# The opening of a Fourier filter with a layer pair behind it: filter read directly, first unit with plain products, weight conversion moved

## The chip, the core and the metric

The kernel runs on one core of a Trainium2 chip. The metric is the time of one execution on the device in microseconds; three runs of the kernel before gave 2558.02, 2558.45 and 2562.6, median 2558.45. The profile is of one further execution. Its engines are TensorE (PE, with PEld for its weight loads), VectorE (DVE), ScalarE (ACT), GpSimd (POOL) and SyncE (SP); SP and POOL issue nearly all transfers.

## The reference

Eight sequences of 3008 tokens with 256 channels are filtered in the frequency domain, and every token then goes through two layers with an ELU between them:

```python
X = np.fft.rfft(x, axis=1)                       # x: (8, 3008, 256)
F = (filt_r + 1j * filt_i)[None, :, :]           # 1505 frequencies x 256
y = np.fft.irfft(X * F, n=x.shape[1], axis=1).astype(np.float32)
x = y.reshape(8 * 3008, 256)
h = x @ w_in                                     # 256 -> 2048
g = np.where(h > 0.0, h, np.exp(np.minimum(h, 0.0)) - 1.0)
return (g @ w_out).astype(np.float32)            # 2048 -> 256
```

The two weight matrices arrive as 64-bit floats, the rest as 32-bit floats.

## The kernel before, in words

**The transform.** 3008 = 47 x 64. A sequence is read as 47 rows of 64 tokens, and row n1 is paired with row 47 - n1, which makes 24 pairs (`H`), in six tiles of four pairs. The first step (`a_first` for batch 0, `a_unit` after that) is a transform of length 64 in a tile, by products with a table. The second is the transform of length 47 across the rows (`b_first`, `b_unit`); it gives the frequencies in groups. In each group DVE multiplies by the filter (`products`, four steps of 128 x 512). Then come the way back (`bi_first`, `bi_unit`), a trip through DRAM (`y_write`, `y_read`; the scratch tensor is `yd`), and a last product with a table (`n_unit`, tile `psn`), after which the rows lie transposed for the layers.

**The layers.** Work is cut into units: a batch has six (m = 0 to 5), each of four row blocks of at most 256 tokens, and a unit runs in four quarters q, each with 512 of the 2048 hidden features. One quarter of one unit is one step of the big loop, here called a quarter; there are 8 x 6 x 4 = 192. A quarter's two products are done as 2 x 2 block products by a scheme with seven products in place of eight (Strassen's, in Winograd's form): `up_steps` gives seven steps of PE for the first layer, `down_steps` seven for the second, and the second runs one quarter behind. Sums of input blocks (`n_sums`), of weight blocks (`w_sums`, four DVE additions a pair of weight tiles) and of ELU outputs go with it. The ELU of a block is two ACT steps (Relu, Exp) and one DVE step. First-layer results lie in four PSUM banks that are handed out and given back in the order of the program (`bank`, `banks`).

**The weights.** 16 tiles of 128 x 512 (k = 4q + j; j = 0, 1 of the first layer, 2, 3 of the second) are fetched as pairs of 32-bit words (`w_fetch`, 512 KB each) and converted by hand: `w_split` (two DVE steps cut mantissa and exponent out of the upper word), `w_float` (four ACT steps: low word, mantissa, two for the exponent), `w_join` (DVE: sign, sum, product into the weight tile).

**The opening, batch 0.** In the order of the program: POOL fetches weight tiles 1 to 3 and then sorts the filter, DRAM to DRAM, into `fd` with 28 transfers (`f_arrange`), later reads it into the tile `ff` with 16 (`f_read_first`, one pair for each of eight groups). SP fetches tile 0, the six x tiles and their tables, further weight tiles in between. PE does `a_first` for each x tile as it comes; its results go to the tiles `zt`. `t_first` transposes them for a group (32 transposes ahead of the loop, 8 behind each of the first four groups). The filter loop runs over g = 0 to 9: `b_first(g)`, products, `bi_first(g - 2)`, `y_write_first(g - 2)`. Tiles 0 to 6 are converted ahead of the loop, 7 to 10 in it, 8 to 13 partly and wholly behind it, 12 to 15 to their end during the first unit. Tiles of x, of `zq`, `rq` and of the result buffers serve as room for weights in between.

**The order behind it** is written out by hand: `plan` names, for each quarter and each of four places in it, what is put there (place 2 and 3 inside the first half, 0 in the middle, 1 behind the quarter's end); `opens` names quarters that begin with a second-layer step. Every engine runs its instructions strictly in this order. `f_pairs` builds, in four pieces during quarters 1 to 4, a second DRAM copy of the filter (`fp`) for batches 1 to 7. The first step of batch 1 (`x_unit`, `a_unit`, `z_write`) stands in quarters 2 to 4, its second (`b_unit`, which needs `z_read`) at the end of quarter 6.

[...]

Of the kernel before, what the change touches and what calls it, by code (L numbers as in the profile page):

```python
# [26 lines left out]
P = 128  # L27
# [14 lines left out]
def _make_tables():  # L42
# [78 lines left out]
    tw = np.ascontiguousarray(tn[:, 0:8].reshape(4, K2, 8, 2, 2, 32).transpose(1, 0, 2, 4, 3, 5)).reshape(P, 8, P)  # L121
# [12 lines left out]
def kernel(  # L134
# [49 lines left out]
    fd = fdp.tile([NG, 2, 48, 2, 2, D], FP32, name="fd")  # L184
# [105 lines left out]
    def t_first(g):  # L290

        t = t2s[0, g] = t4p.tile([P, 4, D], FP32, tag="t4", name="tf") if g % 4 > 1 else t2[:, g % 4]
        for j in range(2):
            i = j + 2 * (g % 2 if g < 4 else 0)
            ps = psO.tile([P, 2, 256], FP32, tag="po%d" % i, name="po%d" % i)
            for u in range(2):
                k = 4 * g + 2 * j + u
                for dh in range(2):
                    nc.tensor.transpose(ps[0:ROWS, u, ts(dh, P)], zt[k // 16][dh][:, ts(k % 16, ROWS)], eye)  # L299
            nc.scalar.activation(out=t[0:ROWS, 2 * j:2 * j + 2, :], in_=ps[0:ROWS], func=AXT.Copy)  # L300
# [19 lines left out]
    def f_read_first(g, t):  # L320
        for a, r in enumerate((LO, HI)):
            nc.gpsimd.dma_start(t[r].rearrange("p c u d -> p (c u d)"), fd[g, a].rearrange("q c u d -> q (c u d)"))
# [12 lines left out]
    def products(re, im, f, sr, si, p, q):  # L335

        nc.vector.tensor_tensor(out=sr, in0=re, in1=f[:, 0], op=ALU.mult)
        nc.vector.tensor_tensor(out=si, in0=re, in1=f[:, 1], op=ALU.mult)
        nc.vector.scalar_tensor_tensor(out=p, in0=im, scalar=-1.0, in1=f[:, 1], op0=ALU.mult, op1=ALU.mult)
        nc.vector.tensor_tensor(out=q, in0=im, in1=f[:, 0], op=ALU.mult)  # L340
# [144 lines left out]
    def y_read(b, m, *parts):  # L485
        t = t4s[b, m] = t4p.tile([P, 4, D], FP32, tag="t4", name="t4")
        for k in parts or (slice(0, K2),):
            if whole(b, m):
                r = slice(4 * k.start, 4 * k.stop)
                nc.sync.dma_start(t[r], yds[b].rearrange("k (p i) d -> (k p) i d", p=4)[r, 4 * m:4 * m + 4, :])  # L490
                continue
            for r in range(2):
                o = 64 * r
                nc.sync.dma_start(t[o + 2 * k.start:o + 2 * k.stop].rearrange("q i d -> q (i d)"),
                                  yds[b][k.start + r:k.stop:2].rearrange("k (p i) d -> k p (i d)", p=4)
                                  [:, :, 4 * m * D:4 * m * D + 4 * D])
# [9 lines left out]
    def n_whole(b, m):  # L506
# [10 lines left out]
        b11, b12, b21, b22 = rows  # L517
        t = yp.tile([P, 2, 256], FP32, tag="yb", name="yb")[:, :, 0:h]
# [42 lines left out]

    COMBO = {1: 0, 2: 2, 3: 6, 4: 3, 5: 4, 6: 5, 7: 1}
# [5 lines left out]
    def up_steps(b, m, q):  # L568

        h = half(m)  # L570
# [82 lines left out]
    def down_steps(b, m, q):  # L653
        h = half(m)
# [82 lines left out]
    def w_fetch(k, queue=nc.gpsimd):  # L737
        q, j = divmod(k, 4)

        if k in (3, 4, 14, 15):  # L740
            wd = t2[:, k % 11 - 3].rearrange("p u d -> p (u d)")
        elif k == 10:
            wd = t1p.tile([P, XC, D], FP32, tag="t1", name="wd").rearrange("p u d -> p (u d)")
        elif k in (6, 7, 8, 9):
            wd = xp.tile([P, 2, 2, D], FP32, tag="xc", name="wd").rearrange("p k u d -> p (k u d)")
        else:
            wd = fbufs[{5: 0, 11: 0, 12: 1, 13: 2}.get(k, k)].rearrange("p c u d -> p (c u d)")
# [14 lines left out]
    def w_split(k):  # L762
        m, e, f, l = wts[k] = wtmp[{9: 2, 10: 1, 11: 0, 12: 3, 13: 4, 15: 5}.get(k, k % 2)]
# [4 lines left out]
    def w_float(k, *parts):  # L768
        m, e, f, l = wts[k]
        ef = e.bitcast(FP32)  # L770
        steps = ((l, wds[k][:, :, 0], AXT.Identity, 2.0 ** -52, 0.0), (f, m, AXT.Identity, 2.0 ** -20, 1.0),
                 (ef, e, AXT.Relu, -8.0, edges[:, 0:1]), (e, ef, AXT.Relu, -1.0, edges[:, 1:2]))
        for i in parts or range(4):
            o, x, func, scale, bias = steps[i]
            nc.scalar.activation(out=o, in_=x, func=func, scale=scale, bias=bias)

    def w_join(k, parts=(0, 1)):
        q, j = divmod(k, 4)
        m, e, f, l = wts[k]
        if 0 in parts:  # L780
            nc.vector.scalar_tensor_tensor(out=e, in0=wds.pop(k)[:, :, 1], scalar=0x80000000, in1=e,
# [320 lines left out]
```

## Time and profile before

| | |
|---|---|
| median of three runs | 2558.45 us |
| profiled execution, its own time / span | 2560.57 / 2558.6 us |
| PE, DVE, ACT busy | 99%, 81%, 60% |
| last rows of x landed | 39.63 us |
| filter loop's first product (psr) | 48.43 us |
| first unit's first product (psn) | 85.68 us |
| end of the second batch's psa behind quarter 3 | 137.37 us |

The span is cut into stages by landmarks in the timeline of PE: the first step's products have the tile `psa`, the transposes and the way back `po`, the second step `psr` and `psi`, the last table product `psn`, the layers' first products `phs`, `pha`, `phd`. L numbers are lines of the kernel before. In the table of stretches the columns are: the stretch and its length, then busy time and count for PE, PEld, DVE, ACT and POOL, then the granted clock, the share of the DMA engines and GB/s. In a timeline, square brackets hold idle time ahead of the row and what ended it.

### The profile page before, as it was taken

The page shows a single profiled execution, that of the slowest core. Times are in us where ns is not written, and L with a number is a line of the kernel's source. Part 1 is how long each engine was busy: PE and PEld are TensorE (multiplying, and loading weights), DVE is VectorE, ACT ScalarE, POOL GpSimd, SP SyncE. Part 2 cuts the span into 40 slices and gives each one's busy share as a digit, 9 for nine tenths or more (in the row PEclk, how much of TensorE's full clock was granted, in tenths as well). Part 3 has the DMA queues.
Part 4 walks back from the last instruction along what each step waited for, and adds up shares of the span by engine and source line. Part 5 has one row for each costly group of instructions (what it writes and reads, how often), then busy time and mean ns, then how long its engine had stood idle before and what let it go on. Part 6 is the DMA issues. An engine that isn't in the chain of part 4 may idle for free.

```text
span 2558.6 us, 43997 instructions
## 1 busy us (share of the span) xinstructions
PE 2522.3 (99%) x16690; PEld 2164.8 (85%) x16690; DVE 2066.1 (81%) x3577; ACT 1544.9 (60%) x2716; POOL 160.2 (6%) x315
## 2 busy tenths in 40 slices
PE   6999999999999999999999999999999999999999
PEld 4788889888898888988889888888888888898888
DVE  6978887788878888788887888778897788876766
ACT  7765556655566565665566656565656655555555
POOL 5001000010000000000000000000100011000000
PEclk9999999999999999999999999999999999999999
DMA  9672213522133231433215231343213322110010
GB/s 281 178 189 65 62 39 81 130 67 69 44 102 100 67 69 40 121 82 72 57 44 150 64 80 36 77 122 81 60 41 85 84 63 69 36 46 18 19 28 17
DMA packets 228295, 200.62 MB, mean 78 GB/s; under 512 B 127174, under 2 KB 200406, under 8 KB 228084
## 3 DMA queue, kind: packets, MB, share of 16 engines
q1 hardware_dynamic: 213588, 166.93, 26.6%
q0 software_dynamic: 14000, 30.44, 4.3%
q8 instruction: 131, 2.15, 0.4%
q14 instruction: 80, 0.66, 0.1%
q10 hardware_dynamic: 496, 0.46, 0.1%
HBM read 125.86 MB, written 78.12 MB: 80 GB/s over the span
## 4 chain that ended last, share of the span: by engine, by line
PE 96%; DMA 2%; DVE 1%; ACT 0%; issue 0%; SPq 0%; DVEq 0%; ACTq 0%
PE po L665 45%; PE phs L583 25%; PE phd L583 13%; PE pha L583 6%; PE psn L535 2%; PE psa L237 2%; PE pf L388 1%; PE pv L460 1%; DMA xc<-in_x_dram 1%; DMA x<-in_x_dram 0%; PE po L333 0%; PE po L299 0%; DMA yd<-t 0%; PE psr L333 0%; DMA t<-yd 0%
## 5 line engine op out<-in xcount | busy, mean ns | idle before, releaser
L665 PE MATMUL po<-g,wo 128*128 128x256 f32 (+1 forms) x5376 | 1317.6, 377 | 0.0
L665 PEld LDWEIGHTS po<-g,wo 128*128 128x128 f32 x5376 | 1010.7, 190 | 165.8 <-issue 49.6
L594 ACT ACTIVATE g<-phs 128x512 f32<-128x512 f32 (+1 forms) x576 | 338.8, 588 | 737.1 <-PE phs L583 735.7
L601 ACT ACTIVATE e<-e 128x512 f32<-128x512 f32 (+1 forms) x768 | 477.2, 621 | 24.4
L605 DVE SCALAR_TENSOR_TENSOR g<-e,g 128x512 f32<-128x512 f32 (+1 forms) x576 | 387.3, 672 | 13.8 <-ACT e L601 13.4
L591 DVE TENSOR_TENSOR g<-phd,g 128x512 f32<-128x512 f32 (+1 forms) x384 | 258.7, 674 | 165.1 <-ACT e L601 107.7
L583 PE MATMUL phs<-y,wi 128*128 128x256 f32 (+1 forms) x1536 | 388.4, 375 | 0.0
L583 PE MATMUL phd<-y,wi 128*128 128x256 f32 (+1 forms) x1504 | 380.3, 375 | 0.0
L600 ACT ACTIVATE e<-g 128x512 f32<-128x512 f32 (+1 forms) x576 | 354.4, 615 | 34.1 <-DVE g L591 26.7
L583 PEld LDWEIGHTS phs<-y,wi 128*128 128x128 f32 x1536 | 291.9, 190 | 33.4 <-ACT g L594 0.2
L583 PEld LDWEIGHTS phd<-y,wi 128*128 128x128 f32 x1504 | 284.8, 190 | 35.1 <-DVE g L591 2.6
L605 DVE SCALAR_TENSOR_TENSOR g<-e,phs 128x512 f32<-128x512 f32 (+1 forms) x192 | 129.9, 677 | 115.5 <-ACT e L601 115.5
L583 PE MATMUL phs<-yt,wi 128*128 128x256 f32 (+1 forms) x768 | 193.8, 375 | 0.9 <-ACT g L594 0.9
L583 PE MATMUL phs<-yb,wi 128*128 128x256 f32 (+1 forms) x768 | 193.8, 375 | 0.6 <-ACT g L594 0.6
L583 PE MATMUL pha<-yb,wi 128*128 128x256 f32 (+1 forms) x736 | 185.9, 375 | 0.0
L600 ACT ACTIVATE e<-phs 128x512 f32<-128x512 f32 (+1 forms) x192 | 112.3, 585 | 111.9 <-PE phs L583 111.8
L591 DVE TENSOR_TENSOR g<-pha,g 128x512 f32<-128x512 f32 (+1 forms) x192 | 129.3, 673 | 45.5 <-PE pha L583 45.5
L583 PEld LDWEIGHTS phs<-yt,wi 128*128 128x128 f32 x768 | 145.7, 190 | 17.8 <-ACT g L594 1.2
L583 PEld LDWEIGHTS phs<-yb,wi 128*128 128x128 f32 x768 | 143.9, 190 | 19.3 <-ACT g L594 1.0
L327 POOL DMA_DIRECT2D fall<-fp x224 | 110.5, 501 | 721.9 <-DVE r L433 696.7
L583 PEld LDWEIGHTS pha<-yb,wi 128*128 128x128 f32 x736 | 139.8, 190 | 16.1
L642 DVE TENSOR_TENSOR g<-g,g 128x512 f32<-128x512 f32 (+1 forms) x192 | 130.7, 681 | 6.7
(170 smaller groups left out, 2066.3 us busy)
## 6 DMA issues: line engine op xcount, KB each, us to landing
yd<-t SPq DMA_DIRECT2D x127, 192.0 KB
t<-yd SPq DMA_DIRECT2D x92, 256.0 KB
z<-t SPq DMA_DIRECT2D x84, 256.0 KB
fall<-fp POOLq DMA_DIRECT2D x224, 96.0 KB, 3.0
t<-z SPq DMA_DIRECT2D x224, 96.0 KB
out_dram<-o SPq DMA_DIRECT2D x624, 32.0 KB
xc<-in_x_dram SPq DMA_DIRECT2D x84, 128.0 KB
xc<-in_x_dram SPq DMA_DIRECT2D x161, 64.0 KB
```

Source lines behind the costliest of these rows:

```text
L237: nc.tensor.matmul(p[o:o + 64, u, :], w[r, u, o:o + 64], src[r, u, :], start=True, stop=True)
L327: nc.gpsimd.dma_start(t[32 * a:32 * a + 24].rearrange("p c u d -> p (c u d)"), fp[g, a].rearrange("q c u d -> q (c u d)"))
L388: nc.tensor.matmul(pf[p][1][32 * a:32 * a + 32, js, :], fb[r, v, :], t2[r, js, a, :], start=True, stop=True, tile_position=(32 * p, 32 * a))
L535: nc.tensor.matmul(o, t[r, i - 4 * m, ds(dh * P + 64 * c, 64)], w[r, i - 4 * m, :], start=True, stop=True)
L583: nc.tensor.matmul(ps[:, a, 0:h], w_in[q][:, COMBO[n], a, :], y[n], start=start and a == 0, stop=True, skip_group_check=True)
L591: nc.vector.tensor_tensor(out=g[o], in0=i0, in1=i1, op=ALU.add)
L594: nc.scalar.activation(out=g[o], in_=i0, func=AXT.Copy)
L600: nc.scalar.activation(out=e, in_=src, func=AXT.Relu, scale=-1.0)
L601: nc.scalar.activation(out=e, in_=e, func=AXT.Exp, scale=-1.0)
L605: nc.vector.scalar_tensor_tensor(out=g[n], in0=es[n], scalar=1.0, in1=src, op0=ALU.subtract, op1=ALU.max)
L642: nc.vector.tensor_tensor(out=b12, in0=b22, in1=b12, op=ALU.subtract)
L665: nc.tensor.matmul(po[i][:, u, 0:h], w_out[q][:, COMBO[n], a, :], g[n][:, a, :], start=q == 0 and a == 0 and n in (1, 3, 6, 4), stop=True, ...
```

## The change

Four things are changed together.

1. The filter no longer goes through `fd`. `f_read_first(k, n)` reads frequencies k to k + n - 1 of each half straight from the inputs into `ff`, for (0, 4), (4, 4) and (8, 8): 26 transfers on SP, behind x and the two tables, and 12 of seven rows on POOL. A group now holds frequencies 2g, 2g + 1 and 16 + 2g, 16 + 2g + 1; transposes, the table `tw` and `y_read` of batch 0 follow that order (four transfers in place of two for m = 2 to 5). `f_pairs` reads the inputs too.
2. Weights: tiles 0 to 2 come on POOL first of all, tile 3 on SP behind x tile 3, tiles 4 to 8 behind the filter, 9 during the loop, 10 to 15 behind the read of yd. The conversion has one ACT step less (`w_join` does the mantissa's scaling). Ahead of the loop tiles 0 to 3 are converted, none in it; tile 4 begins before the last eviction, 4 to 7 and half of 8 are behind the loop, the rest are in quarters 0 to 2.
3. The first unit (b = 0, m = 0) is done with eight plain block products per layer and quarter in two sets of steps (`plain_ups`, `plain_downs`). It needs no sums. The weights' sums go to quarters 2 to 7, all on DVE; one set was on POOL before.
4. The first step of batch 1 moves to quarters 3 to 5.

```diff
-    def f_read_first(g, t):
-        for a, r in enumerate((LO, HI)):
-            nc.gpsimd.dma_start(t[r].rearrange("p c u d -> p (c u d)"), fd[g, a].rearrange("q c u d -> q (c u d)"))
+    def f_read_first(k, n):
+        for c, src in enumerate((filt_r, filt_i)):
+            for a in range(2):
+                o, row, e = 64 * a, 16 * a + k, 1 if k == a == 0 else 0
+                nc.sync.dma_start(ff[o:o + 48:2, c, k:k + n].rearrange("q k d -> q (k d)"),
+                                  raw(src, row, [[64 * D, 24], [1, n * D]]))
+                for j, m, queue in ((0, 16, nc.sync), (16, 7, nc.gpsimd)):
+                    queue.dma_start(ff[o + 2 * j + 1:o + 2 * (j + m):2, c, k + e:k + n],
+                                    raw(src, 64 * (j + 1) - row - e, [[64 * D, m], [-D, n - e], [1, D]]))
...
+    def plain_ups(b, m, q):
...
+        def step(i, j, k):
+            if k == 0:
+                held[i, j] = bank("php")
+            n, ps = held[i, j]
+            for a in range(2):
+                nc.tensor.matmul(ps[:, a, 0:h], w_in[q][:, 2 * k + i, a, :], rows[k][j],
+                                 start=k == a == 0, stop=True, skip_group_check=True)
+            if k == 1:
+                src = ps[:, :, 0:h]
+                e = ep.tile([P, 2, 256], FP32, tag="e", name="e")[:, :, 0:h]
+                nc.scalar.activation(out=e, in_=src, func=AXT.Relu, scale=-1.0)
+                nc.scalar.activation(out=e, in_=e, func=AXT.Exp, scale=-1.0)
+                nc.vector.scalar_tensor_tensor(out=g[i, j], in0=e, scalar=1.0, in1=src, op0=ALU.subtract, op1=ALU.max)
+                banks.append(held.pop((i, j))[0])
...
+    def plain_downs(b, m, q):
...
+        def step(i, j, e):
+            for a in range(2):
+                nc.tensor.matmul(po[e][:, j, 0:h], w_out[q][:, 2 * i + e, a, :], g[i, j][:, a, :],
+                                 start=q == i == j == a == 0, stop=True, skip_group_check=True)
...
-        steps = ((l, wds[k][:, :, 0], AXT.Identity, 2.0 ** -52, 0.0), (f, m, AXT.Identity, 2.0 ** -20, 1.0),
-                 (ef, e, AXT.Relu, -8.0, edges[:, 0:1]), (e, ef, AXT.Relu, -1.0, edges[:, 1:2]))
+        steps = [(l.bitcast(FP32), l, AXT.Identity, 2.0 ** -52, 1.0),
+                 (ef, e, AXT.Relu, -8.0, edges[:, 0:1]), (e, ef, AXT.Relu, -1.0, edges[:, 1:2])]
...
-            nc.vector.tensor_tensor(out=f, in0=f, in1=l, op=ALU.add)
+        nc.vector.scalar_tensor_tensor(out=f, in0=m, scalar=2.0 ** -20, in1=l, op0=ALU.mult, op1=ALU.add)
...
-            f_arrange()
-            w_fetch(0, nc.sync)
...
+            for k, n in ((0, 4), (4, 4), (8, 8)):
+                f_read_first(k, n)
...
-                if g == 1:
-                    w_split(9)
-                if g == 2:
-                    w_join(7)
-                    w_sums(7, nc.gpsimd)
-                if g == 5:
-                    w_split(10)
-                if 3 <= g < 6:
-                    w_fetch(g + 8, nc.sync)
+                if g == 3:
+                    w_fetch(9)
+                for k in {NG: (4,), NG + 1: (5, 6, 7)}.get(g, ()):
+                    w_split(k)
+                    w_float(k)
+                    if k > 4:
+                        w_join(k - 1)
...
+        for quad, place, fn, k in ((0, 2, w_float, 8), (0, 2, w_split, 9), (0, 2, w_join, 8), (0, 2, w_float, 9),
+                                   (0, 0, w_split, 10), (0, 0, w_join, 9), (0, 0, w_float, 10),
+                                   (0, 1, w_split, 11), (0, 1, w_join, 10), (0, 1, w_float, 11),
+                                   (1, 2, w_split, 12), (1, 2, w_join, 11), (1, 2, w_float, 12),
+                                   (1, 0, w_split, 13), (1, 0, w_join, 12), (1, 0, w_float, 13),
+                                   (1, 1, w_split, 14), (1, 1, w_join, 13), (1, 1, w_float, 14),
+                                   (2, 2, w_split, 15), (2, 2, w_join, 14), (2, 2, w_float, 15), (2, 0, w_join, 15),
+                                   (2, 1, w_sums, 1), (2, 1, w_sums, 3), (3, 2, w_sums, 5), (3, 0, w_sums, 9), (3, 1, w_sums, 7),
+                                   (5, 1, w_sums, 13), (6, 1, w_sums, 11), (7, 1, w_sums, 15)):
...
-                for c, s in enumerate((2, 2, 3, 3, 4, 4) if b == 1 else (0, 0, 3, 3, 4, 4)):
+                for c, s in enumerate((3, 3, 4, 4, 5, 5) if b == 1 else (0, 0, 3, 3, 4, 4)):
```

## The prediction

> **What bounds the kernel now.** I read the busy shares first, then the busy time in stretches of the start, then the chain that ended last for the same start, then the timelines of PE, ACT and SP there.
>
> ```profile
> PE 2522.3 (99%) x16690; PEld 2164.8 (85%) x16690; DVE 2066.1 (81%) x3577; ACT 1544.9 (60%) x2716; POOL 160.2 (6%) x315
> ```
> ```profile
> 0.00:10.00 10.00, 0.00 (x0) 0.00 (x0) 5.74 (x9) 8.64 (x9) 6.71 (x17) 1.00 0.80 221
> 10.00:20.00 10.00, 4.88 (x21) 4.65 (x22) 8.34 (x18) 7.10 (x14) 5.62 (x10) 1.00 1.06 301
> 20.00:30.00 10.00, 5.00 (x32) 4.68 (x31) 4.80 (x12) 5.50 (x13) 5.03 (x9) 0.94 1.06 328
> 30.00:40.00 10.00, 5.01 (x32) 4.68 (x32) 4.59 (x9) 6.17 (x13) 3.31 (x6) 0.84 1.05 354
> ...
> 60.00:70.00 10.00, 10.00 (x94) 5.16 (x90) 7.86 (x14) 7.98 (x14) 3.41 (x5) 1.00 0.71 189
> ```
> ```profile
> 28.15 11.48 DMA x<-in_x_dram
> ...
> 39.76 3.77 PE psa L280 x16
> ...
> 44.08 4.42 PE po L299 x31
> 48.50 0.36 PE psr L333
> ...
> 80.53 4.05 DMA t<-yd
> 84.58 1.10 issue
> 85.68 2.74 PE psn L513 x16
> ```
>
> PE is busy 99% of the span, and from about 138 us on it has no gap worth naming. So the change can move the time in two ways only: when the first layer unit starts (psn at 85.68), and how much PE work or idling lies behind that point. Up to 39.63 us the start is transfer: the DMA share (the last column but one) is full, PE half idle, and the chain ends in the last rows of x. From 48.43 to 77.2 the filter loop runs with PE full; then rows go to DRAM and back (77.2 to 85.68). Three rows of the timelines carry the rest:
>
> ```profile
> 92.33 1.02 PE L583 MATMUL phs<-yb,wi 128*128 128x224 f32 x4 [0.63 <-ACT g L594]
> 93.20 0.92 PE L583 MATMUL phd<-y,wi 128*128 128x224 f32 x4
> ...
> 119.46 1.02 PE L583 MATMUL phd<-yb,wi 128*128 128x224 f32 x4 [1.66 <-DVE g L591]
> ```
> ```profile
> 153.69 3.61 SPq L311 DMA_DIRECT2D z<-t  x4
> 160.62 3.50 SPq L317 DMA_DIRECT2D t<-z  x8
> ```
>
> One product step (four records of 224 columns) takes 0.757 us where steps follow each other (105.26, 106.01 and so on). Even before, the first unit waits for ACT and DVE.
>
> **The change, part by part.** The sum is made against the profiled execution: span 2558.6, its own time 2560.57, 2.1 above the median 2558.45. The shift is applied to the median.
>
> *Transfers of the start: -13.8.* By 39.63 us the kernel before moves 2.21+3.01+3.28+0.963x3.54 = 11.9 MB (rate columns). That holds the DRAM-to-DRAM sorting of the filter (28 POOL transfers) and eight weight tiles. Afterwards x needs ahead of its last rows only weight tiles 0 to 3 (4x0.524), x (3.08), its tables (1.57) and the twelve small POOL filter pieces (62x7 rows of 1 KB, 0.44): 7.19 MB. At the rates of the rows, 2.21 in the first ten, 3.01 in the second, the last 1.97 at 341 GB/s (mean of the next two), x is there at 25.8 us instead of 39.63. Ends: 24.1 if everything after 10 us ran at 354, 30 at 250. I take 25.8, since it copies the same queues at the same stage.
>
> *x to filter loop: -1.0.* After the last x rows come 16 products (3.77), 32 transposes (4.42) and their evictions: 8.8 us. The granted clock was 0.50 at 40 to 45 us; an earlier set of 16 took 2.02. With x tiles closer together PE idles less: between 0 and -2.1 (1.75, and 0.3 of transposes); I take the middle.
>
> *The filter itself: 0.* 26 SP and 12 POOL pieces (24 to 192 KB) replace 28 + 16 POOL transfers. SP issues them behind x and the two tables, at 0.4 to 0.6 us each, and each waits for the transfer eight places before it (before, too: SP stood 3.3 us in front of L755 for an x transfer): the first ten (needed for groups 0 and 1) are in about 5 us after x, the next eight 9.5, the last eight 14. The products need them 9, 15 and 24 us after x (49.62, 55.40 and 64.78 less 39.63, less the 1 of above). The cover is 4 to 10 us; if it is gone, the excess is the price. Behind the pieces on SP stand tiles 4 to 8 and the first yd write, due only 18 us after x.
>
> *Filter loop: -0.4.* The conversions taken out of it are 3.4 us of DVE (split 9, join 7, split 10), but in groups 2 to 4 PE sets the pace (3.8 us a group) and DVE waits, 1.33 us in front of 64.78. Only split 10 (0.67, at 69.76) lies ahead of the last products. Against that, the three ACT steps of tile 4 stand in front of the last eviction: +0.3. The yd write, read back and psn stay 8.5.
>
> So psn starts 15.2 earlier, at 70.5.
>
> *First unit plain: +6.05.* Per quarter 8 product steps up and 8 down instead of 7 and 7; 4x2x0.757 = 6.05 us, all on PE.
>
> *Conversions of tiles 8 to 15 under the first unit: +0.3.* A tile costs ACT 0.57+1.36 = 1.93 (the 0.52 step on m is gone), DVE 0.67 + 1.95. Tiles 4 to 7 fit in the 10 us in which rows travel; DVE ends some 3.6 us behind the start of psn, its first layer result is due 5.4 behind it. Then I listed the queues from the rows' durations: each block costs ACT 1.16, DVE 0.54; quarter 0 has four blocks and tiles 8 to 11 (12.4 us of ACT against 6.05 of PE), quarter 1 tiles 12 to 14, quarter 2 tile 15. PE runs ahead by the four banks, then waits 1.9 us in the psn of the second unit and 3.0 at the start of quarter 2, and is free of ACT after that. Idle up to the end of quarter 3 comes to 6.3 with the slow first step (1.61); before it was 51.7 (85.68 to 137.37) less 45.4 of work, also 6.3. I put 0.3 for edges. Ends: -2 (all hidden but the bank waits) and +14 (below).
>
> *Sums of the tiles, 32 DVE adds moved to quarters 2 to 7, four of them off POOL: +0.3.* 1.68 us a set, after the quarter's own work; a DVE burst of 5 us cost 1.66 at 119.46. Ends 0 and 1.7. The four sums of the unit's rows and seven adds at its end go away, on DVE and hidden.
>
> *Second batch's first step one quarter later: +1.5.* Its z rows are now written at the end of quarter 5 and needed at the end of quarter 6: 14 steps of 0.863, 12.1 us after the last psa. Before, psa ended at 150.8 and the reads of z were issued 160.62 to 164.1, plus 3.0 (the median landing of 96 KB pieces): 16 us, under two quarters of cover. In a later batch the reads began 7.5 instead of 9.8 after psa. So 13.7 to 16 against 12.4: 1.3 to 3.6; less SP work stands ahead of it now (no filter pair), so 1.5.
>
> *Reordered rows of yd, two SP transfers more for four units, four more for the pairs: 0*, off the path; SP has whole quarters for them.
>
> Sum: -13.8 -1.0 -0.4 +6.05 +0.3 +0.3 +1.5 = -7.05, 2558.45 to 2551.4.
>
> **The rivals.** *Conversions starve the first unit (slower).* Place: ACT's queue in quarters 0 to 2, with results of products queued behind conversion steps that wait for DVE's splits, and DVE's joins that wait for ACT. For it: 92.33 and 119.46 show such waits already; now eight tiles instead of three lie there. Against: plain blocks need one ACT pair and one DVE step each, no sums. If nothing of ACT's 8x1.93 and of five waits of 0.85 for splits were covered, PE would idle 19.7 instead of 5.4: +14.3, 2565.7. It decides from 12 us of extra idling.
>
> *x comes earlier.* Without the DRAM-to-DRAM sorting, everything after 10 us runs at 354 GB/s: x at 24.1, 2549.7. For it: 402 and 398 in 20 to 25 and 30 to 35 us; against: 254 in between. [...]
>
> *x comes no earlier than 30 us.* If SP alone gets 250 GB/s out of the engines, the start gains 4.2 less: 2555.6. For it: windows of 5 us at 241 and 254 exist; against: 398 and 402 as well.
>
> *The filter pieces come late.* The 192 KB reads of the filter before took 6.3 us to land, the sorting's 128 KB pieces 8.5. With eight in flight, 26 pieces take 3.25 rounds, 20 to 28 us: the last would be up to 4 us late, 2555.4. Mind that loaded engines gave these values, and after x they are free. [...]
>
> **How the numbers follow.** Forecast as summed 0.55, x earlier 0.15, starved unit 0.14, x late 0.09, filter late 0.07. What can be told from no change is 0.2%, 5.1 us, so faster is below 2553.3. The forecast's own range is 2548.8 (clock warm, z rows in time) to 2554.9 (z 3.6, adds 1.7), with 0.04 of its chance above 2553.3. Faster: 0.51 + 0.15 = 0.66; same: 0.04 + 0.09 + 0.07 = 0.20; slower 0.14. The range leaves out most of the starved unit and the far end of the early x: 2546 to 2560.
>
> **What would show it.** Last x rows landing near 26 us; psn near 70.5; no conversion rows between the products of the filter loop and their spacing 3.8, then 2.6; products in the loop with no wait for a DMA; PE idle of 2 and 3 us before the second unit's psn and quarter 2, behind DVE; a wait of 1 to 2 us in front of the first pf products. The forecast is wrong if PE idles over 12 us more in the first three quarters, if x lands after 29 us, or if products wait for ff.

## The result, and the profile after

The kernel after is slower: median 2571.13 us of five runs against 2560.76 us of five runs of the kernel before beside them, ratio 1.0045 (95% interval 1.003 to 1.006), that is +10.4 us. The forecast was 2551.4, range 2546 to 2560. The profiled execution of after took 2572.86 us, its span is 2571.1; the spans differ by 12.5.

In the views of after and of the experiments, L numbers are lines of that run's own kernel. The first line of the page, then the busy time in stretches of the start (columns as before: PE, PEld, DVE, ACT, POOL, clock, DMA share, GB/s), then the chain that ended last in the start, all of the kernel after:

```profile
PE 2531.1 (98%) x16722; PEld 2171.4 (84%) x16722; DVE 2049.2 (80%) x3542; ACT 1529.3 (59%) x2688; POOL 137.3 (5%) x276
```
```profile
10.00:20.00 10.00, 7.50 (x32) 6.97 (x32) 5.09 (x10) 3.99 (x10) 4.04 (x7) 1.00 1.08 227
20.00:30.00 10.00, 4.04 (x32) 3.72 (x32) 2.32 (x6) 6.56 (x16) 0.00 (x0) 1.00 1.08 228
30.00:40.00 10.00, 7.46 (x42) 7.27 (x43) 2.37 (x6) 3.25 (x10) 0.00 (x0) 0.66 0.58 143
40.00:50.00 10.00, 10.00 (x91) 6.93 (x89) 5.35 (x9) 5.77 (x12) 0.00 (x0) 1.00 0.53 147
```
```profile
18.42 13.53 DMA t<-tf_t
32.09 6.42 PE psa L279 x32
...
50.88 6.98 DMA wd<-in_moe_w_in_dram
57.87 5.47 DMA yd<-t
63.45 0.60 ACT t L373
```

The DMA engines are as full as before (share 1.08 from 10 to 30 us, 1.05 and 1.06 in before from 10 to 40), but they move 227 and 228 GB/s where the kernel before moved 301 to 354. The table of the last two x tiles lands at 31.95, and the transfer eight places behind it on SP starts at 31.97. The filter piece eight places behind the last x rows starts at 34.31, by which I put their landing at 34.3; the forecast had 25.8. Then the chain shows something that was not there before: in the middle of the filter loop a weight tile and the first yd write end the wait.

Where PE waited behind the start, from its timeline (idle time and what ended it in brackets):

```profile
64.10 1.46 PE L340 MATMUL po<-rq,gs 48*64 48x512 f32 x5 [1.57 <-ACT t L373]
...
106.62 1.16 PE L522 MATMUL psn<-tn,t 128*128 128x128 f32 x8 [1.58 <-DVE g L600]
110.50 3.35 PE L593 MATMUL php<-y,wi 128*128 128x224 f32 x8 [2.72 <-DVE g L600]
...
168.14 1.13 PE L656 MATMUL phd<-yb,wi 128*128 128x256 f32 x4 [1.98 <-DVE g L664]
189.50 1.13 PE L740 MATMUL po<-g,wo 128*128 128x256 f32 x4 [0.77 <-DVE wo L883]
194.10 1.13 PE L656 MATMUL phs<-yb,wi 128*128 128x256 f32 x4 [0.88 <-ACT g L667]
205.60 1.99 PE L740 MATMUL po<-g,wo 128*128 128x256 f32 x8 [1.74 <-DVE wo L883]
```

The first lies in the filter loop, behind the late yd write. The next two are the waits that the prediction had named (1.9 and 3.0 there). The last four are new, 5.4 us together. From the first product with the tile `pv` on (it belongs to the second batch's frequency work) both kernels run alike: in before it comes at 215.83, in after at 227.81, and these 12.0 us are all but 0.5 of the 12.5 between the spans.

So I read the runs by five landmarks, in us. "last psa" is the start of the last unbroken run of psa products: in before the set of x tile 5 alone, in after those of tiles 4 and 5 together. "q3" is the psa product behind quarter 3.

| run | last psa | psr | psn | psr to psn | psn to q3 | psn to pv | median of the run, ratio to before (95%) |
|---|---|---|---|---|---|---|---|
| before | 39.76 | 48.43 | 85.68 | 37.25 | 49.80 | 130.15 | 2560.8 |
| after | 32.09 | 42.55 | 83.44 | 40.89 | 54.18 | 144.37 | 2571.1, 1.0045 (1.0030 to 1.0060) |
| e4_plain_only | 40.67 | 46.76 | 83.38 | 36.62 | 49.80 | 132.73 | 2562.5, 1.0011 (1.0003 to 1.0020) |
| e3_places | 31.10 | 41.49 | 82.19 | 40.70 | 51.48 | 141.53 | 2570.8, 1.0047 (1.0033 to 1.0060) |
| e7_step_back | 32.33 | 42.51 | 84.79 | 42.28 | 56.33 | 139.24 | 2568.4, 1.0032 (1.0019 to 1.0044) |
| e13_interleave | 24.90 | 34.33 | 74.22 | 39.89 | 54.11 | 144.33 | 2565.6, 1.0021 (1.0012 to 1.0030) |
| e15_late_pool | 29.42 | 39.80 | 76.92 | 37.12 | 54.29 | 144.69 | 2568.1, 1.0031 (1.0018 to 1.0043) |
| e16_all | 25.36 | 33.23 | 71.02 | 37.79 | 56.15 | 139.07 | 2556.3, 0.9986 (0.9977 to 0.9995) |

In before, e4, e7 and e16 a psa set of quarter 2 lies inside "psn to q3" (2.0 us, 121.93 to 123.9 in before); in the others it does not. One execution is not exact: e3, e7 and e8 (42.75) have the code of after up to psn and lie between 40.70 and 42.75 in "psr to psn", and psn to pv lies between 143.3 and 146.2 in the ten runs that leave everything behind psn as in after. (e4 keeps the opening of before except for the weights' sums, which leave it; its psn came 2.3 us earlier.)

### The profile page after: what moved, and what is told of

The parts are those of the page before. It is cut to its first block, busy times and chain, and to the rows that moved or that the text cites. A ratio compares the mean times of both kernels' runs of the same rounds, so it can differ in the third digit from the quotient of the medians.

```text
span 2571.1 us, 44012 instructions
## 1 busy us (share of the span) xinstructions
PE 2531.1 (98%) x16722; PEld 2171.4 (84%) x16722; DVE 2049.2 (80%) x3542; ACT 1529.3 (59%) x2688; POOL 137.3 (5%) x276
## 4 chain that ended last, share of the span: by engine, by line
PE 95%; DMA 2%; ACT 1%; DVE 1%; SPq 0%; issue 0%; ACTq 0%; DVEq 0%
PE po L740 44%; PE phs L656 25%; PE phd L656 12%; PE pha L656 6%; PE psn L547 2%; PE psa L236 2%; PE pf L396 1%; PE pv L468 1%; PE po L616 1%; DMA xc<-in_x_dram 1%; PE php L593 1%; DMA t<-tf_t 1%; PE po L340 0%; DMA yd<-t 0%; DMA wd<-in_moe_w_in_dram 0%; PE psa L279 0%
## 5 line engine op out<-in xcount | busy, mean ns | idle before, releaser
L740 PE MATMUL po<-g,wo 128*128 128x256 f32 (+1 forms) x5264 | 1293.1, 377 | 2.5 <-DVE wo L883 2.5
L740 PEld LDWEIGHTS po<-g,wo 128*128 128x128 f32 x5264 | 989.4, 190 | 168.3 <-issue 48.8
L667 ACT ACTIVATE g<-phs 128x512 f32<-128x512 f32 (+1 forms) x564 | 332.2, 589 | 735.0 <-PE phs L656 733.5
L674 ACT ACTIVATE e<-e 128x512 f32<-128x512 f32 (+1 forms) x752 | 467.9, 622 | 23.8
L678 DVE SCALAR_TENSOR_TENSOR g<-e,g 128x512 f32<-128x512 f32 (+1 forms) x564 | 379.5, 673 | 13.2 <-ACT e L674 12.8
L656 PE MATMUL phs<-y,wi 128*128 128x256 f32 (+1 forms) x1504 | 380.0, 375 | 0.0
L673 ACT ACTIVATE e<-g 128x512 f32<-128x512 f32 (+1 forms) x564 | 347.6, 616 | 33.2 <-DVE g L664 26.3
L656 PEld LDWEIGHTS phs<-y,wi 128*128 128x128 f32 x1504 | 285.6, 190 | 33.0
```

Source lines behind the costliest of these rows:

```text
L656: nc.tensor.matmul(ps[:, a, 0:h], w_in[q][:, COMBO[n], a, :], y[n], start=start and a == 0, stop=True, skip_group_check=True)
L667: nc.scalar.activation(out=g[o], in_=i0, func=AXT.Copy)
L673: nc.scalar.activation(out=e, in_=src, func=AXT.Relu, scale=-1.0)
L674: nc.scalar.activation(out=e, in_=e, func=AXT.Exp, scale=-1.0)
L678: nc.vector.scalar_tensor_tensor(out=g[n], in0=es[n], scalar=1.0, in1=src, op0=ALU.subtract, op1=ALU.max)
L740: nc.tensor.matmul(po[i][:, u, 0:h], w_out[q][:, COMBO[n], a, :], g[n][:, a, :], start=q == 0 and a == 0 and n in (1, 3, 6, 4), stop=True, ...
```

## Experiments on the start: why x moves slowly

**Longer runs.** The reversed rows of x in one run of 4 KB instead of four of 1 KB.

```diff
-        nc.sync.dma_start(t[HALVES[1], u:XC, :], raw(x, N1 - XC * c - u, [[N1 * D, 64], [-D, XC - u], [1, D]]))
+        nc.sync.dma_start(t[HALVES[1], u:XC, :].rearrange("p u d -> p (u d)"),
+                          raw(x, N1 - XC * c - XC + 1, [[N1 * D, 64], [1, (XC - u) * D]]))
```

> The kernel after, but the reversed rows of x (half of each x tile) are read in forward order as runs of 4 KB instead of rows of 1 KB: the same bytes, the same number of transfers, the wrong order of those rows, so that this part of the computation is changed. Theory (the start's transfers go slowly because half of x moves as 1 KB rows, 228 GB/s with all engines full): the rate between 10 and 30 us rises to at least 300 GB/s, the last psa starts at 25 to 27 us instead of 32.09 and psr at 36 to 38 instead of 42.55. Rival (SP's queue, the tables or the small pieces on POOL hold x up): the rate stays below 250 GB/s and the last psa above 30.5 us.

Measured: 238 GB/s from 10 to 20 us, last psa at 30.58, one time of 2570.75. From 10 to 32 us it moved 2309 packets where after moved 3038, at practically the same rate. My first theory, short packets, fell.

**One transfer of 128 partitions, two queues, four transfers of 128 rows.** Of these three edits of `x_load_first` the first reads other rows for the upper half, the second moves `HALVES[1]` to `nc.scalar.dma_start` at the start, the third is

```diff
+        for v in range(XC):
+            k = XC * c + v
...
+                nc.sync.dma_start(t[:, v, :], raw(x, k, [[(N1 - 2 * k) * D, 2], [N1 * D, 64], [1, D]]))
```

> The kernel after, but each tile of x comes as one transfer that fills all 128 partitions with runs of 4 KB, in place of two that fill 64 each; the bytes are the same, the rows in the upper half are other rows of x, so that this part of the computation is changed. Forward rows in two transfers (the packet experiment) were no faster, 238 GB/s. Theory (a transfer that writes 64 partitions uses half of what the way into SBUF has, and the queue works through one transfer after the other): the rate between 12 and 27 us rises above 290 GB/s, near the 390 that the weight tiles reached from 54 to 57, and the last psa starts at 25 to 28 us. Rival (the side it is read from, rows 47 KB apart, or the mix with the small filter pieces sets 230 GB/s): no faster, last psa at 30.5 to 32.5.

> The kernel after, with the upper half of each x tile issued by ScalarE at the start, on its own queue, instead of by SP; nothing else is changed. If filling 64 partitions at a time is what holds x back, both halves now come side by side: last psa at 26 to 29 us, psn at 78 to 81, total 2566 to 2569. If it is the reading side or the number of small rows, the last psa stays at 30.5 to 32.5 and the total at 2569 to 2573.

> The kernel after, with each x tile read by four transfers of 128 rows of 1 KB (one for each of the four rows of a pair, lower and upper half of the partitions together) instead of two of 64 partitions: the right rows, twice as many transfers (24), smaller runs. One transfer of 128 partitions a tile brought the last psa from 32.1 to 24.6 us and psn from 83.4 to 76.3; two halves on two queues did not raise the rate (240 to 256 GB/s). Theory (the width of a transfer, 128 against 64 partitions, sets the rate): above 280 GB/s from 10 to 20 us, last psa at 25 to 28, psn at 76 to 80, total 2564 to 2568. Rival (it was the halved number of transfers, or the rows of another sequence, that made it fast): about 230 GB/s, last psa at 31 or later (SP issues 24 transfers in place of 12), total 2570 to 2575.

The stretch from 10 to 20 us of e5, and the one from 20 to 30 of e9:

```profile
10.00:20.00 10.00, 9.17 (x57) 8.56 (x55) 5.32 (x10) 7.63 (x20) 4.11 (x7) 1.00 1.06 324
```
```profile
20.00:30.00 10.00, 3.75 (x16) 3.48 (x16) 1.99 (x3) 3.18 (x7) 0.00 (x0) 0.92 0.21 70
```

e5: last psa at 24.55, psn at 76.32, one time of 2565.6: as the theory had it. e6: 256 GB/s, last psa at 31.36, 2572.0 (ratio 1.0044, 1.0029 to 1.0059). Its last psa waited for ACT (1.46), which had issued transfers for 9 us before it came to its own work. The upper halves were all issued by 9.2 us and the last lower half at 19.11, so that the halves moved side by side only at first: e6 misses its expectation, but does not decide the question. e9 missed both expectations: 2619.6, ratio 1.0233. The DMA share fell to 0.21. The rate in forty slices of the stretch from 10 to 30 us of e9:

```profile
GB/s 47 49 45 103 47 166 244 281 121 157 123 117 53 45 47 47 45 53 41 47 47 49 45 47 47 47 47 47 47 47 47 47 51 150 338 98 47 47 47 47
```

Where x moves alone, it moves at 47 GB/s. e9's access has an outermost dimension of 2, where after's has 64 and e5's 128; but it also has only one row of 1 KB for a partition, and twice the transfers of after. Which of these makes the rate, e9 alone does not show.

**Width against number of transfers.** e13 puts the two halves of a tile on even and odd partitions, with the table's rows permuted to match; e14 cuts e5's transfer in two, again over 128 partitions, so that there are as many transfers as in after.

```diff
+    tf = np.ascontiguousarray(tf.reshape(2, 64, H, P).transpose(1, 0, 2, 3)).reshape(P, H, P)
...
-        nc.sync.dma_start(t[HALVES[0]].rearrange("p u d -> p (u d)"), raw(x, XC * c, [[N1 * D, 64], [1, XC * D]]))
-        nc.sync.dma_start(t[HALVES[1], u:XC, :], raw(x, N1 - XC * c - u, [[N1 * D, 64], [-D, XC - u], [1, D]]))
+        nc.sync.dma_start(t[0:P:2].rearrange("p u d -> p (u d)"), raw(x, XC * c, [[N1 * D, 64], [1, XC * D]]))
+        nc.sync.dma_start(t[1:P:2, u:XC, :], raw(x, N1 - XC * c - u, [[N1 * D, 64], [-D, XC - u], [1, D]]))
```

> The kernel after, with the two halves of an x tile on even and odd partitions (the table's rows follow) instead of partitions 0 to 63 and 64 to 127: the same 12 transfers of 64 rows, the same bytes and runs, the right values. If 64 adjacent partitions are what makes x slow, the rate from 10 to 30 us rises from 228 above 280 GB/s, last psa at 25 to 28 us instead of 32.1, psn at 76 to 79, total 2564 to 2567. If the number of transfers or of rows in each sets it, nothing changes: last psa 30.5 to 32.5, total 2569 to 2573.

> The wide experiment (each x tile as one transfer over 128 partitions, part of the rows being others than they should, last psa at 24.6) with that transfer cut in two, each over all 128 partitions with runs of 2 KB: 12 transfers of 256 KB as in after. If width sets the rate, it stays fast: last psa at 24 to 26.5. If it was the halved number of transfers, it is slow again: 30 to 32.5.

The same stretch in e13, then in e14:

```profile
10.00:20.00 10.00, 7.70 (x48) 7.37 (x48) 3.61 (x7) 6.19 (x15) 2.81 (x5) 1.00 1.08 292
```
```profile
10.00:20.00 10.00, 8.97 (x49) 8.71 (x49) 5.28 (x10) 6.08 (x14) 3.94 (x7) 1.00 1.06 310
```

e13: last psa at 24.90, psn at 74.22, 2565.6. e14: last psa at 25.09, one time of 2565.33. The same 12 transfers, bytes and runs are fast as soon as each is spread over the whole range of partitions, and 12 wide transfers are nearly as fast as six (last psa 25.09 and 24.55). What held x at 227 and 228 GB/s is that each transfer wrote 64 adjacent partitions: in e13 these alone differ in x's transfers, and the same ten microseconds bring 292. What in the hardware makes adjacent partitions slower, no run shows.

## Experiments on SP: weight tiles 4 to 8

SP's queue in after, rows for the first filter piece, the one that waits for the last x rows and the last one, for tiles 4 and 5, and for the first yd write:

```profile
27.63 0.90 SPq L323 DMA_DIRECT2D ff<-in_filt_r_dram  x1
...
34.31 0.76 SPq L323 DMA_DIRECT2D ff<-in_filt_i_dram  x1
...
49.50 0.65 SPq L326 DMA_DIRECT2D ff<-in_filt_i_dram  x1
50.25 1.00 SPq L832 DMA_DIRECT2D wd<-in_moe_w_in_dram  x2
...
56.59 3.44 SPq L381 DMA_DIRECT2D yd<-t  x4
```

The 26 pieces hold SP for 22.6 us. From 34.31 on, when it no longer waits for x, 21 of them follow each other without a pause for 15.9 us; the DMA share is 0.58 from 30 to 40 us and 0.53 from 40 to 50.

**Fewer pieces; tiles on POOL; tiles on POOL behind x.** The edits (e2, e10, and e15, which has e10's edit too):

```diff
-            for k, n in ((0, 4), (4, 4), (8, 8)):
+            for k, n in ((0, 16),):
```
```diff
-                w_fetch(k)
+                w_fetch(k, nc.gpsimd)
```
```diff
+            nc.gpsimd.tensor_tensor(out=spare, in0=xs[0, 5][:, 3, 0:2], in1=xs[0, 5][:, 3, 2:4], op=ALU.add)
```

> The kernel after, with the filter read in one group of 16 frequencies a half instead of three: 10 transfers on SP and 4 on POOL in place of 26 and 12, the same bytes. Theory (SP, which spent 22.6 us issuing 26 pieces at 0.87 each, was late with weight tiles 4 to 8 and so with the first yd write): SP is through with the filter by 42 us instead of 50.2, tiles 4 to 8 land before 50, the wait of 6.2 us of ACT at the first yd tile and PE's 1.57 at 64.10 go away, the filter loop takes 29 us instead of 32.2, and psn starts at 79.5 to 81 if the first product is not late; total 2 to 4 us less than after (2567 to 2569). Rival (the issue time goes with the rows moved, not with the transfers, or the larger pieces land later than the first group's product needs them at 42.5): SP is no earlier, or the products wait for ff; psn at 83 or later and the total as after (2571) or up to 4 more.

> The kernel after, with weight tiles 4 to 8 issued by POOL, which has nothing else to issue then, instead of by SP behind the 26 filter pieces. The one-group experiment could not decide this point, because the larger filter pieces themselves came 5 to 8 us too late for the first products. Theory (the loop's 1.6 us of waiting and its length of 32.2 us come from tiles 4 to 8 and the first yd write standing behind the pieces on SP): first yd write issued by 52 us instead of 56.6, no wait of PE for ACT's t in the loop, psn 2 to 4 us earlier (79.5 to 81.5), total 2567 to 2569. Rival (with 2.5 MB moved ahead, the filter pieces come later than the products need them): products wait for ff, psn at 83 or later, total 2571 or more.

> The kernel after, with weight tiles 4 to 8 issued by POOL, behind one small addition on POOL that needs the last x rows, so that they move neither against x nor behind the 26 pieces on SP. Theory (SP's lateness costs the loop 4 us): psr at 41.5 to 43 as after, psr to psn 36.5 to 38 us instead of 40.9, psn at 78.5 to 80.5, total 2566.5 to 2568.5. Rival (behind x they collide with the filter pieces instead, which then are late for groups 2 to 7): psr to psn 40 or more, total 2571 or more.

e2: SP turned to tile 4 at 40.4, but the rival came true elsewhere: the large pieces landed in 10 and 12.5 us, and the second group waited for them.

```profile
27.45 10.03 DMA ff<-in_filt_r_dram
37.49 12.49 DMA ff<-in_filt_i_dram
50.10 0.70 DVE rq L346
```

psn at 88.85, 2580.6, ratio 1.0082 (1.0069 to 1.0096). The groups of the change are worth having. e10: psr to psn fell from 40.89 to 36.66 as the theory had it, but the last psa came 4.5 us later (36.55, and it was followed by another set), with the tiles now moving against x: psn 83.52, 2574.0, ratio 1.0055 (1.0040 to 1.0070). e15 took both apart: psr to psn 37.12, no wait of PE in the loop, first yd write issued at 50.86 instead of 56.59, 2568.1. SP's lateness with tiles 4 to 8 costs the filter loop and its end about 4 us: psr to psn is 36.27 to 37.79 in e10, e11, e15 and e16, where POOL issues them, and 38.51 to 42.75 in after and in e1, e3, e5, e7, e8, e9, e13 and e14, where they stand on SP as in after. (That psr came 2.7 us earlier than in after, 39.80, with the last x rows there by 31.7, is not explained by this edit; with the opening of after unchanged in what precedes psr, e3, e7 and e8 had it at 41.49, 42.51 and 40.40.)

## Experiments behind psn

**The plain unit alone**, in the kernel before, sums in quarters 2 to 6.

```diff
+                                    (2, 1, w_sums, 1), (3, 2, w_sums, 3), (3, 0, w_sums, 5), (3, 1, w_sums, 9),
+                                    (4, 2, w_sums, 7), (4, 1, w_sums, 11), (5, 1, w_sums, 13), (6, 0, w_sums, 15)):
```

> The kernel before with the plain first unit alone: eight block products a layer and quarter; opening, fetches and conversions of the kernel before; the weights' sums in quarters 2 to 6 on DVE. Theory (the plain unit costs its added products, less the waits of the first three quarters that the missing sums take away): psn at 85.7 as before, the end of quarter 3's psa 4 to 6.5 us later than before's 137.37, total 3.5 to 6.5 above before (2564.3 to 2567.3). Rival 1 (the missing sums free DVE and ACT enough to pay for it): total within 1.5 us of before. Rival 2 (the plain form itself stalls, behind its eight-row products at a lower clock or behind ELU results, as after's 7.6 us suggest): 7 us or more above before.

2562.5 (ratio 1.0011, 1.0003 to 1.0020), 2.7 us above the before measured beside it: between the first rival's 1.5 and the theory's 3.5. In quarters 0 to 3 it cost nothing at all, 49.80 us with and without; up to pv it cost 2.6. Of these 2.6, 0.76 are the last of the added products and 1.01 is a wait at 173.94; sums that stood in the opening of before now lie there too. In before PE had waited 0.63, 0.90, 1.66 and 0.60 us in these quarters, behind ACT and DVE, and its clock stood at 0.64 in the first 4 us; in e4 one wait of 0.81 is left and the clock is 1.00 throughout:

```profile
86.21 7.83 PE L584 MATMUL php<-y,wi 128*128 128x224 f32 x40 [0.81 <-ACT y L514]
```

**Places of the sums and of the moved step.** e3 moves the sums of tiles 11, 13, 15 and one pair of `x_unit`; e7 moves the sums the same way and puts the first step back. e7's edit:

```diff
-                                   (5, 1, w_sums, 13), (6, 1, w_sums, 11), (7, 1, w_sums, 15)):
+                                   (4, 2, w_sums, 11), (5, 1, w_sums, 13), (6, 0, w_sums, 15)):
...
-                for c, s in enumerate((3, 3, 4, 4, 5, 5) if b == 1 else (0, 0, 3, 3, 4, 4)):
+                for c, s in enumerate((2, 2, 3, 3, 4, 4) if b == 1 else (0, 0, 3, 3, 4, 4)):
```

> The kernel after, with the sums of tiles 11, 13 and 15 one to two quarters earlier (quarters 4, 5 and 6) and the first step's second block of products for batch 1 in quarter 5 put into the first half of the quarter instead of its middle. Theory (four places of DVE work cause the waits of PE of 0.77, 0.88, 1.74 and 1.98 us between 168 and 206 us): all four are gone or under 0.3, the first pv comes 4.5 to 5.5 us earlier behind psn than after (144.4 us from psn to pv there), and the total is 2565.5 to 2567. Rival (DVE's work is merely moved, and the same waits come back at other steps): pv within 1.5 us of after, total 2570 to 2572.

> The kernel after, with the first step of batch 1 back in quarters 2 to 4 and the sums of tiles 11, 13, 15 in quarters 4 to 6. The earlier change of places took PE's waits for DVE away, but 3.73 us of them came back in front of psn at 199.75 and 202.68, as waits for rows of yd whose reading stands on SP behind 24 output transfers (11.1 us), these in turn behind the z writes and x loads of the moved step (172 to 184 us). Theory (the moved step sets it, through DVE and then SP): no wait of PE over 1.1 us between 165 and 215 us, psn to pv 136 to 139.5 us (144.4 after, 141.5 with the sums alone), total 2563.5 to 2567.5. Rival (the four reads in place of two for these units, or the conversions' late end, hold SP and DVE up whichever quarter the step is in): psn to pv above 141, total 2568 to 2572.

e3's four waits for DVE were gone, and two new ones stood at the next psn. PE's timeline in e3, then SP's in after and in before:

```profile
199.75 0.30 PE L547 MATMUL psn<-tn,t 64*64 64x64 f32 x2 [1.10 <-DMA t<-yd]
202.68 1.21 PE L547 MATMUL psn<-tn,t 64*64 64x64 f32 x62 [2.63 <-DMA t<-yd]
```
```profile
189.72 11.14 SPq L790 DMA_DIRECT2D out_dram<-o  x24
...
201.37 2.86 SPq L503 DMA_DIRECT2D t<-yd  x4
```
```profile
172.96 11.88 SPq L715 DMA_DIRECT2D out_dram<-o  x24
...
185.36 1.21 SPq L494 DMA_DIRECT2D t<-yd  x2
```

In these timelines SP issues its transfers in the order of the program. In before the 24 output transfers start 1.9 us after their first rows are ready (171.1); in after these are ready at 177.8 and the transfers start 11.9 us later, because the z reads (178.49 on) and x loads of the moved step now stand ahead of them, and the reading of yd stands behind. While DVE held PE up, this did not show; in e3 it took back 3.73 of the 5.4 us (psn to pv 141.5; of the 2.8 less than after, 2.7 come from quarters 0 to 3, whose code is the same, see the clock below). The median did not move. e7 has one wait left between 165 and 215 us (1.00 at 181.86), psn to pv 139.24, 2568.4: a little above the theory's time, with the path behind psn as it said. The moved step and the late sums cost 5.2 us.

**The clock in the first unit.** Behind the wait of 2.72 us the two runs of the same code part. After, then e3, 4 us each, from 1.5 and 0.8 us behind that wait:

```profile
112.00:116.00 4.00, 4.00 (x12) 3.60 (x12) 3.73 (x9) 3.75 (x7) 0.00 (x0) 0.50 0.83 260
```
```profile
110.00:114.00 4.00, 4.00 (x23) 4.00 (x22) 3.76 (x9) 3.15 (x7) 0.00 (x0) 1.00 0.64 200
```

12 products against 23, at a clock of 0.50 against 1.00. In the 48 us behind psn the clock took 3.4 us in after, e13 and e15, 5.1 in e1 and e10, 1.7 in e7 and e11, none in e3, e4 and e16 (sums of 4 us stretches times the missing share). The idle time there is 4.3 in after and 0.8 in e4. So the 6.4 us by which the conversions lengthen this stage in after are about 3.5 of waiting, and the lower clock accounts for the rest. Not every run makes up the 6.4 in this way: in e16 the clock stays at 1.00 and the idle time is 5.2, and the psa set of quarter 2 takes 4.3 us (110.60 to 114.87) against 2.0 in before.

**Conversions spread over quarters 0 to 3.** Two tiles a quarter, each joined ahead of its use, by the list of places; for example

```diff
+                                   (2, 2, w_split, 12), (2, 2, w_join, 11), (2, 2, w_float, 12),
+                                   (2, 0, w_split, 13), (2, 0, w_join, 12), (2, 0, w_float, 13), (2, 1, w_join, 13),
+                                   (3, 2, w_split, 14), (3, 2, w_float, 14),
```

> The kernel after, with the conversions of tiles 9 to 15 spread over quarters 0 to 3 (two tiles a quarter, each joined just ahead of its use) instead of four, three and one in quarters 0 to 2. With the plain unit alone in the kernel before, psn to the end of quarter 3 took 47.9 us, as much as there without it; after takes 54.2 (51.5 and 56.0 in two other runs of the same code). Theory (conversions on ACT and DVE in front of the first unit's ELU cost these 4 to 8 us): the waits of 1.58 and 2.72 in front of the second psn and of quarter 2 are gone or under 0.8, and psn to the end of quarter 3 takes 48.5 to 51.5 us; total 2566 to 2569. Rival (each tile costs its share wherever it stands, ACT and DVE being full through quarter 3): still 53 to 56, the waits only at other places, total 2570 to 2573.

The waits of 1.58 and 2.72 went, psn to q3 fell to 51.82, but 2.31 (`wi`, joined late) and 1.34 came instead, and from there to pv it took 4.0 us longer (94.19 against 90.19). 2576.0, ratio 1.0065 (1.0051 to 1.0079): psn to q3 is just above the theory's range, but the waits came back at other places, as the rival has it, and the total is above both ranges. The trace accounts for 1.6 of the 4.9 us between the medians; the rest I did not find.

## Everything together

e11 joins e9's x, e10 and e7; e12 also converts tiles 4 to 8 between the filter steps.

```diff
-                for k in {NG: (4,), NG + 1: (5, 6, 7)}.get(g, ()):
+                for k in {2: (4,), 3: (5,), 5: (6,), 7: (7,), 8: (8,), NG + 1: (9, 10)}.get(g, ()):
```

> The kernel after with three changes together: x by transfers of 128 partitions, tiles 4 to 8 on POOL, first step of batch 1 in quarters 2 to 4 with the sums of tiles 11, 13, 15 in quarters 4 to 6. By the separate readings psn comes at 74 to 78 us and pv 139 us behind it: pv at 213 to 217, total 2558 to 2562, level with before. If the gains do not add (the filter pieces, now issued earlier against x, or POOL's transfers of weights collide), total 2563 to 2567.

> As the kernel with these three changes, and tiles 4 to 8 converted between the filter steps again (in groups 2, 3, 5, 7 and 8), 9 and 10 behind the last one, so that only 11 to 15 are left for quarters 0 to 2; tiles 4 to 11 come on POOL. Theory (five conversions fit beside the filter steps, where ACT is busy 33 to 58% and DVE 54 to 64%, while under the first unit they cost PE 6 us): the loop no longer than 31 us, psn to the end of quarter 3 at 48.5 to 51 us instead of 54.2, psn to pv 133 to 137, total 2554 to 2558, below before. Rival (conversions cost in the loop what they cost behind it, since DVE or ACT then holds up the products): loop longer by 3 us or more, total no better than with the three changes alone.

Both carry e9's slow x, so their totals (2617.1 and 2621.1) say nothing; their stages do. psr to psn: 36.27 in e11, 41.82 in e12. psn to pv: 139.10 and 133.73. Five conversions put into the loop cost 5.5 us there and save 5.4 behind psn, in one execution each: the rival, and no gain.

e16 joins the interleaved halves of e13, e15 and e7.

> The kernel after with the interleaved halves of x, tiles 4 to 8 on POOL behind x, and the first step of batch 1 in quarters 2 to 4 with the sums moved. If the interleaving brings x to 25 us: psr at 35, psn at 71 to 73, pv 139 behind it, at 210 to 212.5, total 2554.5 to 2557.5, below before. If it does not: psn at 78.5 to 80.5, total 2562 to 2565, above before.

psr at 33.23, psn at 71.02, pv at 210.09, 2556.3: inside the expectation, and 0.14% below before (interval 0.05% to 0.23%). Its waits that are left behind psn, from PE's timeline:

```profile
93.43 2.02 PE L524 MATMUL psn<-tn,t 128*128 128x128 f32 x16 [1.72 <-DMA xc<-in_x_dram]
98.06 1.78 PE L595 MATMUL php<-y,wi 128*128 128x224 f32 x8 [2.60 <-DVE g L602]
...
167.92 1.13 PE L658 MATMUL phd<-yb,wi 128*128 128x256 f32 x4 [1.00 <-DVE g L666]
```

## Why the prediction was wrong, step by step

| step | forecast | measured | from |
|---|---|---|---|
| transfers of the start | -13.8 | -5.3 | last x rows 39.63 to 34.3 |
| x to filter loop | -1.0 | -0.6 | last x rows to psr, 8.8 to 8.2 |
| filter itself, filter loop, end | -0.4 | +3.6 | psr to psn 37.25 to 40.89 |
| first unit plain | +6.05 | +2.6 | psn to pv 130.15 to 132.73 (e4, with the opening's sums moved) |
| conversions under it | +0.3 | +6.4 | 132.73 to 139.1 (e7, e11, e16) |
| sums, second batch's first step, yd reads | +1.8 | +5.2 | 139.1 to 144.4 |
| sum | -7.05 | +12.0 | pv 215.83 to 227.81 |

- *Transfers.* The order, the queues and the full engines were right. The step that failed was to price x "at the rates of the rows": those rows mixed x with DRAM-to-DRAM sorting and weight tiles. In after, where little but x and its tables moves, transfers of 64 adjacent partitions bring 227 and 228 GB/s, and the last x rows land at 34.3. e13 shows that this was all: spread out, they are there by 26.3 (the filter piece that waits for them starts at 26.34), and the forecast had 25.8; its last psa, at 24.90, waited for ACT and no longer for x. The rival "x comes no earlier than 30 us", at 0.09, was the one that came, though its 250 GB/s were still too many; I had argued against it with windows of 398 and 402 from the same mixture. The 354 GB/s from 10 us on, by which the other rival had x there at 24.1, came in no run: once the transfers were wide, e5 moved 358 from 4 to 14 us, against 282 in after, but from 10 to 20 us no run with the new opening had more than its 324.
- *x to filter loop.* This came out near the forecast, but not by a warmer clock: it was 0.66 from 30 to 40 us. The set of tile 4 waited for the table until 32.09, tile 5's stood right behind it, and the two took 6.42 us, so that the last rows landed while PE still worked on tile 4.
- *The filter itself.* No product waited for `ff`; that part was right. Wrong were the 0.4 to 0.6 us of SP for a piece (0.64 to 0.98), and the sentence that the tiles and the first yd write behind them are due "only 18 us after x": the yd write was issued 22.3 us after it (56.59 less 34.31). I had named the queue and the cover, and mis-sized the issue. e15 gives back 3.8 us.
- *The plain unit and the conversions.* Up to quarter 3, which holds seven of the eight added steps, their sum was forecast at 5.6, and 47.80 (49.80 less the psa set) against 54.18 is 6.4. The two waits that the forecast had named came (1.58 and 2.72 for 1.9 and 3.0). Yet taken singly both terms were wrong, and that they add up is in part luck. e4 shows that the unit alone costs nothing there: the waits of before, 3.8 us in these quarters, go away with the sums and the ELU work that the plain unit sheds. The conversions then cost all of the 6.4. The starved first unit, at 0.14 the slower rival, names the place; its price (14.3, "it decides from 12 us") was twice too high. Moving conversions elsewhere did not lower the cost (e8, e12).
- *Sums, first step, yd reads.* The z rows were in time, there is no wait in front of pf at 184.24: the +1.5 was for a wait that did not come. Instead the moved `x_unit` stood ahead of an addition on DVE (1.98), the sums cost 3.4 (ends 0 and 1.7), and behind them SP's queue was late by ten us, which I had put at 0 with "SP has whole quarters". DVE's waits hid SP's lateness, as e3 shows.

Of the 19 us between the sum forecast and the sum measured, 13.0 lie ahead of psn and 6.1 behind it. With x spread and tiles 4 to 8 off SP, e16 has its psn at 71.02, where the forecast had 70.5; with x alone mended (e13) the kernel was still slower than before, 2565.6.

## What to carry to other kernels

A DMA rate read from a stretch holds for that mixture of transfers (301 to 354 GB/s in before were 227 and 228 for x in after); ask of each stream which partitions one of its transfers writes before moving it to another rate, and try halves on even and odd partitions (292 GB/s here) rather than low and high (227). When a unit is changed that waits today, find whose work it waits for: if the change removes that work, added products may be free, and if other work then takes its place, that is the price. On a queue that issues in the order of the program, as SP's did, moving a step moves the transfers behind it (here the output by ten us), and a faster engine ahead may only uncover it.

## What the runs showed of the hardware that I had not expected

- 64 adjacent partitions against 64 every second one: 227 (after) and 292 GB/s (e13) in the same 10 us, DMA share 1.08 in both. The share alone did not tell the rate.
- e9's x, 128 rows of 1 KB in one transfer with an outermost dimension of 2: 47 GB/s over long stretches, share 0.21 from 20 to 30 us.
- A clock of 0.50 for several us behind waits of only 1.58 and 2.72 us: the eight products behind the second took 3.35 us in after. In e3, with 1.46 and 2.72 us of waiting, they took 1.78. Between the two waits stood eight products (1.16 us) in after and in nine other runs (e1, e2, e5 to e7, e10, e13 to e15), where the eight behind the second took 3.00 to 3.36 us, and sixteen in e3 (2.17 us) and in e16 (2.02 us, waits of 1.72 and 2.60), where the clock stayed at 1.00; no run changed this alone, so whether it decides is not shown.
